# Another order of the opening in a fused attention and gated FFN kernel: the second tile joins at the sixth step, conversions rank above attention

## The chip, the cores and the metric

The kernel runs on one core of a Trainium2 chip. The metric is the device time of one execution in microseconds; the time of a kernel is the median of its runs. The engines are named as in the profile: PE (TensorE, matmuls), PEld (its weight loads), DVE (VectorE), ACT (ScalarE), POOL (GpSimd) and SP (SyncE, which issues every DMA here).

## The reference

Attention over keys and values that are averaged over groups of 8 positions, and behind it a gated FFN on the attention's output:

```python
B, H, S, D = 8, 8, 576, 64
k_p = k.reshape(B, H, 72, 8, D).mean(axis=3)          # 72 pooled keys
v_p = v.reshape(B, H, 72, 8, D).mean(axis=3)
scores = q @ k_p.T / sqrt(D)
attn = softmax(scores)                                 # sum + 1e-9
x = (attn @ v_p).transpose(0, 2, 1, 3).reshape(4608, 512)
out = ((x @ w_a) * (x @ w_b)) @ w_out                  # w_a, w_b: 512 x 1536, w_out: 1536 x 512
```

The weights come as 64-bit floating-point numbers; q, k and v as 32-bit ones.

## The kernel before, in words

**Precision.** Every operand of a matmul is split in a high part (a cast on ACT) and a low part (source minus high part, the helper `low_part`, L183, on DVE or POOL). A product is then three matmuls: high by high, high by low, low by high. For the FFN these are L610 to L612 (in) and L632 to L634 (out).

**Tiles and steps.** The 4608 rows of x are nine tiles of 512 columns (`NT`). A tile goes through 12 steps, one for each 128 of the 1536 hidden columns. A step has an "in" (`ffn_in`: 12 matmuls for psa with w_a, 12 for psb with w_b; ACT copies psa to h at L617, DVE multiplies it by psb at L567) and an "out" (`ffn_out`: 12 matmuls into the four accumulators acc). The product h is split in `split_gated` into hh (ACT, L580) and hl (DVE). The "out" of a step comes after the "in" of the next.

**Converting weights.** The weights' words are loaded and turned to 32-bit numbers in place by `convert_weights`, once for each of a, b, o and each of the 12 steps: two ACT operations (L225, L226), three DVE operations (L227, L231, L236), and the load of the next step's words between the last two. Conversion g may not start before step max(g - AHEAD, 0) of the first tile has begun (list `begun`, two slots later for b, four for o). `split_weight` then makes high (ACT, L262) and low part (L183; for a and b of tile 0 on DVE, otherwise on POOL) for each use, at most two of a weight at a time (`room`).

**The second tile.** Tile 1 uses the freshly converted weights of steps LAG to 11 together with tile 0, so that they are split only once for both. Those products h are "kept": stored to DRAM (`later`, L570) and fetched again (`fetch_gated`, L586) when tile 1's "out" steps are due. Steps 0 to LAG - 1 of tile 1 come afterwards, with splits of their own.

**Attention.** Rows are cut in 40 chunks of 128 or 64. `chunk(i)` loads and splits queries, makes scores on PE (L418 for the first nine chunks, L432 and L435 later, whose two parts DVE adds at L438), softmax (maximum L402, subtraction L403, exponential L452 on ACT, sum and reciprocal L454 to L456, scaling L458 mostly on POOL), splits the probabilities (pr, rem: L467, L469, POOL at L183), turns them on PE (ptr, L513, copied by ACT at L514), and multiplies them by the values (po, L548 to L551; xh at L559 and xl at L183). `load_keys(b)` and `load_values(b)` pool a batch's keys (L282, L293, L298) and values (L334, L339, L343, L354, L357, vrem at L183). The first four chunks make tile 0, the next five tile 1.

**The order.** It is planned in Python while the program is written. The FFN's instructions are issued in the list `order`. An "in" takes four slots, an "out" two (IN, OUT). In each slot `Chains.step` resumes the generators that are due, in order of rank, then one generator that waits for PE. A `yield n` lets a chain rest for n slots; `yield PE` queues it for PE. Where the FFN can't go on, `need` runs steps with up to GROUPS chains on PE each. The order of resumption is the order of instructions in each engine's queue; the engines then run by semaphores. Ranks are PRODUCTS, SPLITS, CHUNKS, WEIGHTS, KEYS (L131), the first ahead. Splits are started LEAD_A, LEAD_B, LEAD_O slots before their use, a fetch LEAD_H slots before. A chunk of tiles 2 to 8 is started CHUNK slots before a point spread evenly over the tile before; keys KEYS_AHEAD slots ahead of a chunk, values VALUES_AFTER slots after the keys.

**The opening.** Chunks of tile 0 start EARLY_GAP slots apart, those of tile 1 from SECOND_START on, SECOND_GAP apart; values, keys and conversions at VALUES_START, KEYS_START and WEIGHTS_START; a conversion's first arithmetic comes CONVERT_AFTER slots after its load. The FFN waits for all of tile 0's attention before its first step, and for all of tile 1's before tile 1's first "in":

```python
        for n, (kind, t, *where) in enumerate(order):
            if kind == "in":
                if t == 0:
                    begun.append(chains.now)
                need(lambda: have(t))
```

Of the kernel before, what the change touches and what calls it, by code (L numbers as in the profile page):

```python
# [55 lines left out]

SUMMED = 9

AHEAD = 2

GROUPS = 4


LAG = 4


IN, OUT = 4, 2
LEAD_A, LEAD_B, LEAD_O, LEAD_H = 5, 4, 6, 8


QUERY_GAP, PROBS_GAP, VALUE_GAP = 4, 2, 4
CHUNK = 34
SECOND_GAP, SECOND_START = 3, 14
KEYS_AHEAD, VALUES_AFTER = 18, 16


EARLY_GAP, VALUES_START, KEYS_START, WEIGHTS_START, CONVERT_AFTER = 1, 2, 8, 10, 5


class Chains:  # L80
# [9 lines left out]
    def mark(self, *what):  # L90
        self.done.add(what)

    def wait(self, *marks):
        while not all(m in self.done for m in marks if not isinstance(m[-1], int) or m[-1] >= 0):
            yield 1
# [26 lines left out]
def attn_moe_kernel(ctx: ExitStack, tc: tile.TileContext, q, k, v, vr, wa, wb, wo, out):  # L122
# [5 lines left out]
    chains = Chains()  # L128
    PE = Chains.PE
    mark, wait, done = chains.mark, chains.wait, chains.done  # L130
    PRODUCTS, SPLITS, CHUNKS, WEIGHTS, KEYS = ((x, 0) for x in range(5))  # L131

    def tmp(name, dtype=F32):
        return sb.tile([P, 512], dtype, tag="tmp", name=name, bufs=NTMP)
# [47 lines left out]
    def low_part(eng, lo, src, hi):  # L182
        eng.tensor_tensor(out=lo, in0=src, in1=hi.bitcast(F32), op=ALU.subtract)  # L183
# [23 lines left out]
    def convert_weights(name, j, first):  # L207
# [11 lines left out]
        for f in range(NF):  # L219
# [19 lines left out]

            step = max(f + 1 - AHEAD, 0)  # L240
            while len(begun) <= step or chains.now < begun[step] + 2 * j:
# [9 lines left out]
    def drop(*keys):  # L251
        for key in keys:
            del parts[key]
            held[key[0]] -= 1
# [53 lines left out]
    def load_values(b):  # L308
        vd = vdiag[b % 2]
        vrem = sb.tile([P, NG, 2, 2, D], F32R, tag="vrem", name=f"vrem_{b}")  # L310
        yield from wait(("keys", b, 2), ("values", b - 1))
        vp = sb.tile([P, NK + NG, D], F32, tag="vp", name=f"vp_{b}", bufs=1)
        for x0 in range(0, NK + NG, 2):
            if b == 0:
                vraw = [early_v[:, x, :] if x < NK else early_vr[:, x - NK, :] for x in (x0, x0 + 1)]
            else:
                if x0:
                    yield from wait(("vraw", b, x0 - 2))
                vraw = [sb.tile([P, S], F32, tag="kv", name=f"vraw_{b}_{x0 + j}")[:, :D * POOL] for j in range(2)]
                for j in range(2):  # L320
                    if x0 < NK:
                        nc.sync.dma_start(vraw[j], v[b, :, x0 + j, :])
                    else:
                        nc.sync.dma_start(vraw[j][:NR], vr[b, :, x0 + j - NK, :])
                yield 3
            for j in range(2):
                x, rows = x0 + j, P if x0 < NK else NR
                vv = vraw[j][:rows].rearrange("p (d j) -> p d j", j=POOL)
                if b == 0 and 0 < x < NK:
                    for n in (4, 2, 1):  # L330
                        to = vp[:rows, x].unsqueeze(2) if n == 1 else vv[:, :, :n]
                        nc.gpsimd.tensor_tensor(out=to, in0=vv[:, :, :n], in1=vv[:, :, n:2 * n], op=ALU.add)
                else:
                    nc.vector.tensor_reduce(out=vp[:rows, x], in_=vv, axis=AX.X, op=ALU.add)  # L334
            mark("vraw", b, x0)
            yield 1
        for e in range(2):
            r = slice(e * KM, e * KM + KM)
            nc.scalar.mul(vd[r, :, 0, r], vp[r, :NK], 1.0 / POOL)  # L339

        wide = tmp(f"vwide_{b}").rearrange("p (r j e d) -> p r (j e) d", r=NG, j=2, e=2)
        for r in range(NG):
            nc.vector.scalar_tensor_tensor(  # L343
                out=wide[:NR, r],
                in0=vp[:NR, NK + r].unsqueeze(1).broadcast_to([NR, 4, D]),
                scalar=1.0 / POOL,
                in1=mask[:NR].unsqueeze(2).broadcast_to([NR, 4, D]),
                op0=ALU.mult,
                op1=ALU.mult,
            )  # L350
        wide = wide.rearrange("p r c d -> p (r c d)")
        vrf = vrem.rearrange("p r j e d -> p (r j e d)")
        yield 1
        nc.scalar.copy(vrf[:NR], wide[:NR])  # L354
        for e in range(2):
            r = slice(e * KM, e * KM + KM)
            nc.vector.scalar_tensor_tensor(  # L357
                out=vd[r, :, 1, r],
                in0=vp[r, :NK],
                scalar=1.0 / POOL,  # L360
                in1=vd[r, :, 0, r].bitcast(F32),
                op0=ALU.mult,
                op1=ALU.subtract,
            )
        yield 1
        r = slice(2 * 4 * KR, NR)
        low_part(nc.vector, vrf[r], wide[r], vrf[r])
        yield 1
        vrems[b] = vrem
        mark("values", b)  # L370

    def chunk(i):
        b, o, n = flat[i]
        t, col = divmod(b * S + o, NT)
        first, soon = i < early, t < 2
# [11 lines left out]
        nc.scalar.copy(qh[:, :, :n], qraw[:, :, :n])  # L387
        yield 1
        low_part(nc.gpsimd if first else nc.vector, ql[:, :, :n], qraw[:, :, :n], qh[:, :, :n])
        yield 1 if soon else QUERY_GAP  # L390
        yield from wait(("probs", i - 2))


# [77 lines left out]
        low_part(nc.gpsimd, pr[:n, 1], s[:n, :, :KM], pr[:n, 0])  # L471
        low_part(nc.gpsimd, rem[:n, :, 1], sr, rem[:n, :, 0])
        mark("probs", i)
        yield 1 if soon else PROBS_GAP


        j = block_of[i]
# [47 lines left out]
        mark("turned", i)  # L525
        if i != members[-1]:
            return
        yield 1 if soon else VALUE_GAP
        yield from wait(("values", b))
        if t not in xtiles:  # L530
            xtiles[t] = [sb.tile([P, NK, NT], F32R, tag=x, name=f"{x}_{t}") for x in ("xh", "xl")]
# [58 lines left out]
    def need(ready):  # L590
        for _ in range(1000):
            if ready():
                return
            chains.step(GROUPS)
        raise RuntimeError("no progress")

    def ffn_in(t, f):
        x = t * NF + f
        xh, xl = xtiles[t]
        kept = t == 1 and f >= LAG  # L600
        for name in ("a", "b"):
# [4 lines left out]
            for kk in range(NK):  # L606
# [5 lines left out]
                nc.tensor.matmul(pt, wl[:, c], xh[:, kk], start=False, stop=(kk == NK - 1))  # L612
            if t or f < LAG:
                drop(key)
# [35 lines left out]
    for f in range(NF):  # L650
        order.append(("in", 0, f))
        if f >= LAG:
            order.append(("in", 1, f))
        if f:
            order.append(("out", 0, f - 1, f == 1, False))
    order.append(("out", 0, NF - 1, False, True))
    seconds = [*range(LAG, NF)]
    for f in range(LAG):
        order.append(("in", 1, f))
        if f:  # L660
            order.append(("out", 1, f - 1, False, False))
        order.append(("out", 1, seconds.pop(0), f == 0, False))
    order.append(("out", 1, LAG - 1, False, False))
    order += [("out", 1, f, False, f == NF - 1) for f in seconds]
# [8 lines left out]
    for kind, t, f, *_ in order:  # L673
        x = t * NF + f
# [7 lines left out]
    with tc.manual_schedule():  # L682
# [8 lines left out]
        for i in range(early):  # L691
            chains.start(chunk(i), (CHUNKS[0], i), EARLY_GAP * i)
        for i in range(early, sum(t < 2 for t in tile_of)):
            chains.start(chunk(i), (CHUNKS[0], i), SECOND_START + SECOND_GAP * (i - early))
        chains.start(load_values(0), KEYS, VALUES_START)
        chains.start(load_keys(1), KEYS, KEYS_START)
        chains.start(load_values(1), KEYS, KEYS_START + 1)
        for j, name in enumerate(("a", "b", "o")):
            chains.start(convert_weights(name, j, CONVERT_AFTER + 2 * j), WEIGHTS, WEIGHTS_START)
# [10 lines left out]
        for n, (kind, t, f, *_) in enumerate(order):  # L710
            x = t * NF + f
# [10 lines left out]
        for i in range(len(flat)):  # L722
            b, o, n = flat[i]
            t = tile_of[i]
            if t < 2:
                continue
            since = free if t == 2 else begin_of[t - 1]
            share = (b * S + o + n - t * NT) / NT
            begin_at = since + int((begin_of[t] - since) * share) - CHUNK
            plan.append((begin_at, chunk(i), (CHUNKS[0], i)))  # L730
            if i + 1 < len(flat) and flat[i + 1][0] > max(b, 1):
                plan.append((begin_at - KEYS_AHEAD, load_keys(b + 1), KEYS))
                plan.append((begin_at - KEYS_AHEAD + VALUES_AFTER, load_values(b + 1), KEYS))
# [60 lines left out]
```

## Time and profile before

| what | value |
|---|---|
| median of 3 runs | 1098.72 us (1096.58 to 1099.33) |
| profiled execution | 1099.94 us, span 1098.2 us |
| PE, PEld busy | 1036.8 us (94%), 860.6 us (78%) |
| DVE, ACT, POOL busy | 588.3, 516.3, 505.7 us |
| mean granted PE clock | 0.981 |

A row of the windows names a stretch of the span in us, then for each engine its busy time in it with the number of instructions, the granted clock (1 is full), the mean busy share of the DMA engines, and GB/s. A row of instructions in order of time has start, duration, engine, line, operation, operands and count, and in brackets the engine's idle time ahead of it with what ended it. A row of the groups has busy time and mean ns of one, then the idle time ahead. A "step" below is a step of a tile, a "slot" a slot of the planner.

### The profile page before, as it was taken

The page shows a single profiled execution, that of the slowest core. Times are in us where ns is not written, and L with a number is a line of the kernel's source. Part 1 is how long each engine was busy: PE and PEld are TensorE (multiplying, and loading weights), DVE is VectorE, ACT ScalarE, POOL GpSimd, SP SyncE. Part 2 cuts the span into 40 slices and gives each one's busy share as a digit, 9 for nine tenths or more (in the row PEclk, how much of TensorE's full clock was granted, in tenths as well). Part 3 has the DMA queues.
Part 4 walks back from the last instruction along what each step waited for, and adds up shares of the span by engine and source line. Part 5 has one row for each costly group of instructions (what it writes and reads, how often), then busy time and mean ns, then how long its engine had stood idle before and what let it go on. Part 6 is the DMA issues. An engine that isn't in the chain of part 4 may idle for free.

```text
span 1098.2 us, 13575 instructions
## 1 busy us (share of the span) xinstructions
PE 1036.8 (94%) x4964; PEld 860.6 (78%) x4964; DVE 588.3 (54%) x941; ACT 516.3 (47%) x1035; POOL 505.7 (46%) x425
## 2 busy tenths in 40 slices
PE   4577699999999999999999999999999999999998
PEld 4555588788878888888877888888887888888886
DVE  7879857764685345644566446543557343422112
ACT  3656535445454445544444445444544344443332
POOL 6213100036555554555455455554545555554442
PEclk9878899999999999999999999999999999999999
DMA  6354424413230002200140002100211010001001
GB/s 217 104 148 125 135 88 148 145 43 118 94 127 1 1 2 75 98 1 1 34 149 1 1 1 89 63 1 1 83 54 37 1 58 1 1 1 39 1 1 39
DMA packets 32178, 63.79 MB, mean 58 GB/s; under 512 B 7376, under 2 KB 7376, under 8 KB 32112
## 3 DMA queue, kind: packets, MB, share of 16 engines
q1 hardware_dynamic: 32112, 62.93, 17.9%
q8 instruction: 39, 0.64, 0.2%
q14 instruction: 27, 0.22, 0.1%
HBM read 51.38 MB, written 11.53 MB: 57 GB/s over the span
## 4 chain that ended last, share of the span: by engine, by line
PE 81%; DVE 11%; ACT 3%; DMA 3%; issue 2%; POOL 0%; SPq 0%; DVEq 0%; ACTq 0%; POOLq 0%
PE psa L610 8%; PE acc L632 8%; PE psb L610 8%; PE acc L634 8%; PE acc L633 8%; PE psa L612 8%; PE psa L611 8%; PE psb L612 8%; PE psb L611 8%; PE ptr L513 2%; PE psc L432 2%; DVE vp L334 1%; PE po L550 1%; PE po L548 1%; PE po L551 1%
## 5 line engine op out<-in xcount | busy, mean ns | idle before, releaser
L567 DVE TENSOR_TENSOR h<-psb,h 128x512 f32<-128x512 f32 x108 | 74.6, 690 | 322.0 <-PE psb L612 314.0
L183 POOL TENSOR_TENSOR jlb<-wb_raw,jhb 128x512 fp32r<-128x512 f32 x88 | 114.9, 1306 | 256.1 <-ACT jhb L262 256.1
L183 POOL TENSOR_TENSOR jlo<-wo_raw,jho 128x512 fp32r<-128x512 f32 x108 | 142.4, 1319 | 141.1 <-ACT jho L262 141.1
L617 ACT COPY h<-psa 128x512 f32<-128x512 f32 x108 | 63.5, 588 | 255.2 <-PE psa L612 241.5
L610 PE MATMUL psa<-xh,jha 128*128 128x512 f32 x432 | 175.5, 406 | 0.8 <-DVE xl L183 0.8
L610 PE MATMUL psb<-xh,jhb 128*128 128x512 f32 x432 | 171.8, 398 | 1.4 <-DVE h L567 1.4
L632 PE MATMUL acc<-jho,hh 128*128 128x512 f32 x432 | 172.1, 398 | 0.0
L611 PE MATMUL psa<-xl,jha 128*128 128x512 f32 x432 | 170.9, 396 | 0.0
L612 PE MATMUL psa<-xh,jla 128*128 128x512 f32 x432 | 170.8, 395 | 0.0
L634 PE MATMUL acc<-jho,hl 128*128 128x512 f32 x432 | 169.1, 392 | 0.0
L633 PE MATMUL acc<-jlo,hh 128*128 128x512 f32 x432 | 168.7, 391 | 0.0
L612 PE MATMUL psb<-xh,jlb 128*128 128x512 f32 x432 | 168.6, 390 | 0.0
L611 PE MATMUL psb<-xl,jhb 128*128 128x512 f32 x432 | 168.5, 390 | 0.0
L183 POOL TENSOR_TENSOR jla<-wa_raw,jha 128x512 fp32r<-128x512 f32 x88 | 120.5, 1370 | 77.1 <-ACT jha L262 69.9
L183 DVE TENSOR_TENSOR hl<-h,hh 128x512 fp32r<-128x512 f32 x100 | 92.5, 925 | 32.7 <-ACT hh L580 32.5
L580 ACT CAST hh<-h 128x512 fp32r<-128x512 f32 x100 | 62.2, 622 | 94.2 <-DVE h L567 91.6
L612 PEld LDWEIGHTS psa<-xh,jla 128*128 128x128 f32 x432 | 82.7, 191 | 18.0
L610 PEld LDWEIGHTS psa<-xh,jha 128*128 128x128 f32 x432 | 82.9, 192 | 15.9 <-DVE xl L183 1.0
L634 PEld LDWEIGHTS acc<-jho,hl 128*128 128x128 f32 x432 | 81.4, 188 | 17.6
L612 PEld LDWEIGHTS psb<-xh,jlb 128*128 128x128 f32 x432 | 81.1, 188 | 17.3
L610 PEld LDWEIGHTS psb<-xh,jhb 128*128 128x128 f32 x432 | 81.1, 188 | 17.2 <-DVE h L567 1.8
L611 PEld LDWEIGHTS psa<-xl,jha 128*128 128x128 f32 x432 | 83.0, 192 | 14.6
(102 smaller groups left out, 1701.8 us busy)
## 6 DMA issues: line engine op xcount, KB each, us to landing
out<-y SPq DMA_DIRECT2D x36, 256.0 KB, 2.2
kraw<-in_k SPq DMA_DIRECT2D x28, 288.0 KB, 3.6
qraw<-in_q SPq DMA_DIRECT2D x28, 256.0 KB, 3.7
vraw<-in_v SPq DMA_DIRECT2D x28, 256.0 KB, 3.0
words<-in_wa SPq DMA_DIRECT2D x12, 512.0 KB, 3.6
words<-in_wb SPq DMA_DIRECT2D x12, 512.0 KB, 3.5
words<-in_wo SPq DMA_DIRECT2D x12, 512.0 KB, 3.6
vraw<-in_vr SPq DMA_DIRECT2D x14, 192.0 KB, 2.8
```

The source lines that it names most:

```text
L183: eng.tensor_tensor(out=lo, in0=src, in1=hi.bitcast(F32), op=ALU.subtract)
L432: nc.tensor.matmul(pt[:n, :2 * hk], qh[:, g, :n], kd[:, g].rearrange("p w e s -> p (w e s)"), start=True, stop=False)
L513: nc.tensor.transpose(ptr[:rows, g, :n], src, ident[:n, :n])
L567: nc.vector.tensor_tensor(out=h, in0=pt, in1=h, op=ALU.mult)
L580: nc.scalar.copy(hh, h)
L610: nc.tensor.matmul(pt, wh[:, c], xh[:, kk], start=(kk == 0), stop=False)
L611: nc.tensor.matmul(pt, wh[:, c], xl[:, kk], start=False, stop=False)
L612: nc.tensor.matmul(pt, wl[:, c], xh[:, kk], start=False, stop=(kk == NK - 1))
L617: nc.scalar.copy(h, pt)
L632: nc.tensor.matmul(acc[c], hh[:, cs], wh, start=first, stop=False)
L633: nc.tensor.matmul(acc[c], hh[:, cs], wl, start=False, stop=False)
L634: nc.tensor.matmul(acc[c], hl[:, cs], wh, start=False, stop=last)
```

## The change

Constants of the order are changed, one pair of ranks is swapped, and three rests of the first chunks' chains are told apart for the first and the second tile. AHEAD goes from 2 to 1, GROUPS from 4 to 3, LAG from 4 to 5; LEAD_A, LEAD_O, LEAD_H from 5, 6, 8 to 3, 8, 6; CHUNK from 34 to 33; SECOND_GAP from 3 to 1; VALUES_AFTER from 16 to 14; EARLY_GAP, VALUES_START, KEYS_START, CONVERT_AFTER from 1, 2, 8, 5 to 2, 3, 6, 2. WEIGHTS ranks above CHUNKS. The turns of a chunk of tile 1 come SECOND_PROBS = 3 slots after the split of its probabilities, where it was 1. `load_values` rests between its operations in batches 2 to 7.

```diff
--- before.py
+++ after.py
@@ -56,25 +56,27 @@
 
 SUMMED = 9
 
-AHEAD = 2
-
-GROUPS = 4
-
-
-LAG = 4
+AHEAD = 1
+
+GROUPS = 3
+
+
+LAG = 5
 
 
 IN, OUT = 4, 2
-LEAD_A, LEAD_B, LEAD_O, LEAD_H = 5, 4, 6, 8
+LEAD_A, LEAD_B, LEAD_O, LEAD_H = 3, 4, 8, 6
 
 
 QUERY_GAP, PROBS_GAP, VALUE_GAP = 4, 2, 4
-CHUNK = 34
-SECOND_GAP, SECOND_START = 3, 14
-KEYS_AHEAD, VALUES_AFTER = 18, 16
-
-
-EARLY_GAP, VALUES_START, KEYS_START, WEIGHTS_START, CONVERT_AFTER = 1, 2, 8, 10, 5
+CHUNK = 33
+SECOND_GAP, SECOND_START = 1, 14
+KEYS_AHEAD, VALUES_AFTER = 18, 14
+
+SECOND_QUERY, SECOND_PROBS, SECOND_VALUE = 1, 3, 1
+
+
+EARLY_GAP, VALUES_START, KEYS_START, WEIGHTS_START, CONVERT_AFTER = 2, 3, 6, 10, 2
 
 
 class Chains:
@@ -128,7 +130,7 @@
     chains = Chains()
     PE = Chains.PE
     mark, wait, done = chains.mark, chains.wait, chains.done
-    PRODUCTS, SPLITS, CHUNKS, WEIGHTS, KEYS = ((x, 0) for x in range(5))
+    PRODUCTS, SPLITS, WEIGHTS, CHUNKS, KEYS = ((x, 0) for x in range(5))
 
     def tmp(name, dtype=F32):
         return sb.tile([P, 512], dtype, tag="tmp", name=name, bufs=NTMP)
@@ -332,6 +334,8 @@
                         nc.gpsimd.tensor_tensor(out=to, in0=vv[:, :, :n], in1=vv[:, :, n:2 * n], op=ALU.add)
                 else:
                     nc.vector.tensor_reduce(out=vp[:rows, x], in_=vv, axis=AX.X, op=ALU.add)
+                if b > 1:
+                    yield 1
             mark("vraw", b, x0)
             yield 1
         for e in range(2):
@@ -348,6 +352,8 @@
                 op0=ALU.mult,
                 op1=ALU.mult,
             )
+            if b > 1:
+                yield 1
         wide = wide.rearrange("p r c d -> p (r c d)")
         vrf = vrem.rearrange("p r j e d -> p (r j e d)")
         yield 1
@@ -362,6 +368,8 @@
                 op0=ALU.mult,
                 op1=ALU.subtract,
             )
+            if b > 1:
+                yield 2
         yield 1
         r = slice(2 * 4 * KR, NR)
         low_part(nc.vector, vrf[r], wide[r], vrf[r])
@@ -387,7 +395,7 @@
         nc.scalar.copy(qh[:, :, :n], qraw[:, :, :n])
         yield 1
         low_part(nc.gpsimd if first else nc.vector, ql[:, :, :n], qraw[:, :, :n], qh[:, :, :n])
-        yield 1 if soon else QUERY_GAP
+        yield (1 if first else SECOND_QUERY) if soon else QUERY_GAP
         yield from wait(("probs", i - 2))
 
 
@@ -471,7 +479,7 @@
         low_part(nc.gpsimd, pr[:n, 1], s[:n, :, :KM], pr[:n, 0])
         low_part(nc.gpsimd, rem[:n, :, 1], sr, rem[:n, :, 0])
         mark("probs", i)
-        yield 1 if soon else PROBS_GAP
+        yield (1 if t == 0 else SECOND_PROBS) if soon else PROBS_GAP
 
 
         j = block_of[i]
@@ -525,7 +533,7 @@
         mark("turned", i)
         if i != members[-1]:
             return
-        yield 1 if soon else VALUE_GAP
+        yield (1 if t == 0 else SECOND_VALUE) if soon else VALUE_GAP
         yield from wait(("values", b))
         if t not in xtiles:
             xtiles[t] = [sb.tile([P, NK, NT], F32R, tag=x, name=f"{x}_{t}") for x in ("xh", "xl")]
```

## The prediction

> **What bounds the kernel now.** I read the page first (engine shares, slices), then the windows of PE's stages, then PE's waits, then the instruction rows around each stall. From the page:
>
> ```profile
> span 1098.2 us, 13575 instructions
> PE 1036.8 (94%) x4964; PEld 860.6 (78%) x4964; DVE 588.3 (54%) x941; ACT 516.3 (47%) x1035; POOL 505.7 (46%) x425
> PE   4577699999999999999999999999999999999998
> DVE  7879857764685345644566446543557343422112
> ```
>
> PE is full except in the first five slices, where DVE stands at 6 to 9 tenths. The opening is one regime, all that follows another. The windows of stages, columns PE, PEld, DVE, ACT, POOL busy with counts, granted clock, DMA share, GB/s:
>
> ```profile
> 0.00:52.60 52.60, 27.10 (x144) 24.57 (x145) 43.10 (x79) 26.54 (x60) 25.52 (x35) 0.94 0.53 168
> 52.60:139.76 87.16, 64.60 (x291) 50.76 (x292) 71.64 (x120) 50.74 (x101) 19.93 (x18) 0.83 0.43 128
> 200.00:222.00 22.00, 20.62 (x93) 16.77 (x92) 16.64 (x29) 9.62 (x19) 1.31 (x1) 1.00 0.41 135
> 222.00:318.00 96.00, 95.84 (x472) 80.25 (x471) 59.44 (x100) 48.84 (x100) 48.38 (x38) 1.00 0.24 77
> 318.00:334.00 16.00, 14.14 (x66) 11.37 (x65) 14.41 (x21) 9.70 (x22) 9.42 (x9) 0.89 0.48 156
> 559.00:595.00 36.00, 32.71 (x163) 26.03 (x161) 25.57 (x40) 16.01 (x34) 17.36 (x15) 1.00 0.21 67
> 595.00:826.00 231.00, 231.00 (x1127) 193.71 (x1126) 114.19 (x184) 111.01 (x225) 124.30 (x102) 1.00 0.12 37
> 826.00:850.00 24.00, 21.45 (x111) 16.54 (x109) 18.31 (x26) 10.37 (x23) 11.39 (x10) 1.00 0.05 17
> 850.00:1093.80 243.80, 243.80 (x1148) 203.06 (x1148) 73.99 (x111) 98.14 (x189) 120.02 (x96) 1.00 0.03 12
> ```
>
> At 52.60 the first FFN step starts; about 139.56 the second tile joins (both rows below). Between them PE idles 87.16 - 64.60 = 22.56 us and runs at clock 0.83, while DVE is busy 71.64 of 87.16 (82%). Later PE is full but for four islands: 1.38 us in 200 to 222, 1.86 in 318 to 334, 3.29 in 559 to 595, 2.55 in 826 to 850; 318 to 334 also has clock 0.89, worth 16 x 0.11 = 1.76 us. One attention-free step of 36 matmuls costs 1009.57 - 1001.41 = 8.16 us, so a planner slot (a sixth) is 1.36 us; PE's instructions in order of time:
>
> ```profile
> 52.60 0.79 PE L610 MATMUL psa<-xh,jha 128*128 128x512 f32 x1 [0.77 <-DVE xl L183]
> 139.56 0.63 PE L610 MATMUL psa<-xh,jha 128*128 128x512 f32 x1
> 1001.41 0.39 PE L610 MATMUL psa<-xh,jha 128*128 128x512 f32 x1
> 1009.57 0.39 PE L610 MATMUL psa<-xh,jha 128*128 128x512 f32 x1
> ```
>
> What PE waits for (us in total, times, longest):
>
> ```profile
> PE ptr L513 <- ACT pr L467: 13.9, 4, 5.4
> PE psc L418 <- ACT p L514: 7.0, 3, 4.3
> PE psc L432 <- DVE s L438: 3.8, 4, 1.4
> ```
>
> The first two belong to the opening's attention, each a link of the chain scores, softmax, turn; the third to the islands.
>
> **The change part by part.**
>
> **Second tile joins at step five, not four; conversions run one step ahead, not two.** In the listed order the second tile's first "in" stands behind 5 "in" and 3 "out" of tile 0 (5x4 + 3x2 = 26 slots); after the change behind 6 and 4 (32 slots). So 36 more matmuls, 8.16 us of PE work, lie where PE now idles, and the second tile's attention gets 6 more slots. What DVE pays: the number of conversions ahead of the join. Now conversion g is released at the start of step g-2, after the change at g-1. Windows of L236, the last operation of a conversion, and of L567 (the product), DVE busy and counts:
>
> ```profile
> 0.00:52.60 52.60, 1.38 (x2) 0.94 0.53 168
> 52.60:139.76 87.16, 15.02 (x19) 0.83 0.43 128
> 52.60:139.76 87.16, 3.41 (x5) 0.83 0.43 128
> ```
>
> 2 + 19 = 21 conversions, three weights times seven (steps 0 to 6), precede the join: number 6 is released by step 4. After the change step 5 stands ahead of the join, and releases number 6 as the last. The conversions stay at 21. What DVE gains is one more split of a and b, one product, one split of the product, at the means of the groups by shape:
>
> ```profile
> L183 DVE TENSOR_TENSOR jla<-wa_raw,jha 128x512 fp32r<-128x512 f32 x12 | 8.2, 684 | 0.0
> L183 DVE TENSOR_TENSOR jlb<-wb_raw,jhb 128x512 fp32r<-128x512 f32 x12 | 9.6, 803 | 0.2 <-ACT jhb L262 0.2
> L567 DVE TENSOR_TENSOR h<-psb,h 128x512 f32<-128x512 f32 x108 | 74.6, 690 | 322.0 <-PE psb L612 314.0 <-ACT jho L262 4.4 <-ACT qh L387 2.0
> L183 DVE TENSOR_TENSOR hl<-h,hh 128x512 fp32r<-128x512 f32 x100 | 92.5, 925 | 32.7 <-ACT hh L580 32.5
> ```
>
> 0.684 + 0.803 + 0.690 + 0.925 = 3.10 us. If the join is set by DVE (82% busy), it comes 3.10 us later with 8.16 us more done: 5.06 us gained. Bounds: the whole 8.16 if the 3.10 fall into DVE's own idle time, zero if the stretch grows by a whole step. I take -5.1, as DVE's share is nearer to full. A conversion one step later has its data sooner, since its words load starts in the conversion before it; SP issues the same word loads. Its split is due three slots (4.1 us) after its release, and late by that only if DVE is jammed.
>
> **Smaller consequences of the fifth step.** One store and one fetch of h fewer (seven, not eight): off the path, zero. One more a and b split for tile 1, on POOL: 2 x 1.3 us where POOL is busy 48.38 of 96 (222 to 318); zero, and 2.6 us if that cover went. The fetches are issued two slots before their split, not four:
>
> ```profile
> back<-later SPq DMA_DIRECT2D x8, 256.0 KB, 4.6
> ```
>
> 2 slots are 2.72 us, so ACT can stand 1.88 us at the cast, with the next weight's cast queued behind it. Its user is four slots (5.4 us) off and cast and split take about 1.5 us, so this is covered; zero, and 7 x 1.88 = 13.2 us if nothing covers it.
>
> **Order up to the first step** (early chunks two slots apart, keys at 6, conversions after 2 instead of 5 and ranked above chunks, three PE groups instead of four in a wait, second-tile chunks at 14 to 18 instead of 14 to 26, their turns three slots behind their splits). No instruction is added; SP's loads of keys and words trade places. DVE is busy 43.10 of 52.60, so the order can win at most its 9.50 us of idle time. It can lose what is put ahead: three second-tile chunks, each with two maxima, two subtractions and a sum:
>
> ```profile
> L403 DVE TENSOR_TENSOR s<-psc,m 128x288 f32<-128x288 f32 x14 | 6.4, 457 | 0.9
> L402 DVE TENSOR_REDUCE m<-psc 128x4 f32<-128x288 f32 x14 | 6.3, 450 | 0.5 <-PE psc L418 0.4
> L454 DVE TENSOR_REDUCE z<-s 128x8 f32<-128x576 f32 x32 | 23.7, 742 | 0.8 <-ACT s L452 0.8
> ```
>
> 3 x (2 x 0.457 + 2 x 0.450 + 0.742) = 7.7 us. This is moved, not added, and comes back before the join; the three-slot gap of the turns spares PE a turn that arrives before its probabilities. I take zero between -9.5 and +7.7.
>
> **Value loads in pieces (batches 2 to 7).** DVE now gets their operations in pairs. DVE in the islands:
>
> ```profile
> 322.16 2.73 DVE L357 SCALAR_TENSOR_TENSOR vdiag<-vp,vdiag 64x256 fp32r<-64x256 f32 x2 [0.92 <-ACT vdiag L339]
> 571.77 1.47 DVE L334 TENSOR_REDUCE vp<-vraw 96x64 f32<-96x512 f32 x2 [3.41 <-DMA vraw<-in_vr]
> 830.88 1.77 DVE L183 TENSOR_TENSOR vrem<-vwide,vrem 32x512 fp32r<-32x512 f32 x1
> ```
>
> Behind each pair stand the reduction L438 that frees a scores bank, and the product. With yields between, these go first. 200 to 222 (1.38), 318 to 334 (1.86 + 1.76 of clock), and 826 to 850 without its second stall (2.55 - 1.14 = 1.41) sum to 6.41 us; I take all of it. The remaining 3.29 - 1.12 = 2.17 us at 559 to 577 follow a wait for data (3.41 us of DVE idle); the load keeps its three slots, so it stays. Bounds: zero, and 6.41 + 2.17 = 8.58.
>
> **Leads and phases.** a is split three slots ahead, not five, o eight, not six; chunks start one slot later, a phase shift of one sixth of a step. Same instructions. By slots, POOL now gets jlo, jla, jlb in a row, three slots to one before the "in". With 1.32 us each (row below) they fit their slots, and jla is done about one slot (1.36 us) early: zero. If a chunk's pr (1.3) and remainder push them, PE waits some tenths. What a long run on POOL does is seen at 585:
>
> ```profile
> 585.66 1.29 POOL L183 TENSOR_TENSOR jlb<-wb_raw,jhb 128x512 fp32r<-128x512 f32 x1
> 588.16 1.27 POOL L183 TENSOR_TENSOR pr<-s,pr 64x512 fp32r<-64x512 f32 x1
> 586.14 3.84 DVE L183 TENSOR_TENSOR hl<-h,hh 128x512 fp32r<-128x512 f32 x1 [0.69 <-ACT hh L580]
> 590.39 0.34 PE L432 MATMUL psc<-kdiag,qh 128*64 128x288 f32 x1 [1.12 <-DVE s L438]
> 845.16 0.35 PE L432 MATMUL psc<-kdiag,qh 128*64 128x288 f32 x1 [1.14 <-DVE s L438]
> L183 POOL TENSOR_TENSOR jlo<-wo_raw,jho 128x512 fp32r<-128x512 f32 x108 | 142.4, 1319 | 141.1 <-ACT jho L262 141.1
> ```
>
> hl took 3.84 us instead of 0.69 and PE stalled 1.12 us. The Trainium skill, page "SBUF — State Buffer", section "Who interferes with whom", says that a DVE instruction with two SBUF inputs and a GpSimd instruction that reads SBUF exclude each other for the whole instruction; by that rule the three splits in a row keep such DVE work waiting in every step, which speaks against this change, and the sum would be that of the last rival below instead of -11.5. The row agrees for this place; the product h, one of whose inputs is PSUM, has mean 690 over 108. I take zero because hl is due when the run of splits has ended; now it falls beside jlb.
>
> **Sum.** -5.1 - 6.4 = -11.5 us on the profiled execution's 1099.94 (span 1098.2 and 1.7 around it) gives 1088.4; its run lies 1.2 above the median 1098.72, and against that median I predict 1087.2.
>
> **The rivals.**
>
> *The opening only moves its idle time* (the second tile's last chain, not DVE, ends last at the join; the two opening waits, 13.9 and 7.0, speak for it; the 6 slots more for that chain against): -6.4, 1092.3.
>
> *The islands stay* (POOL runs or data, not pairs, make them): -5.1, 1093.6.
>
> *Nothing happens*: first step later by up to 7.7 and islands elsewhere: -11.5 + 7.7 = -3.8 at most, 1095 to 1099. DVE at 82% before 52.60 speaks for it.
>
> *More goes*: the step fits wholly into idle time (8.16), all value stalls (8.58) and the two run stalls (1.12 + 1.14): -19.0, 1079.7.
>
> *Slower: POOL runs stall every chunk.* Three splits in a row, with pr and its remainder ahead of them, hold DVE's subtraction L403 or ql, and through them L438: 1.12 us at each of 31 later chunks is +34.7 (40 chunks less the nine of the first two tiles); less 11.5, it is +23, 1122. It decides from 11 stalls on (11.5 / 1.12 = 10.3), and from 14 on the kernel is measurably slower. For it: the row at 586. Against: only two such stalls now, although POOL has such runs at each chunk, and DVE has half its time free (114.19 of 231.00).
>
> **How the numbers follow.** Forecast 0.38 (its own range 1083 to 1091), more 0.10, opening moves 0.13, islands stay 0.11, nothing 0.12, slower 0.16. Faster by over 0.3% (3.3 us, about what a measurement tells from no change): 0.38 + 0.10 + 0.13 + 0.11 = 0.72; same 0.12; slower 0.16. The range 1077 to 1104 leaves out half of the slower case and a little of "more".
>
> **What would show it.** Right: 7 conversions of each weight and 6 products before the second tile's first matmul; that matmul about 3 us later than 139.56 if the first step starts near 52.6; PE full at the value loads of batches 2, 3 and 7; PE-free stretches still at the fifth batch's value load. Wrong: a first step after 57; hl or L403 with means above 1.5 us and PE waits on L438 at most chunks; a wait of L612 for jla in each step; seven ACT waits for fetched h in tile 1's second half with PE idle behind them.

## The result, and the profile after

The changed kernel takes 1070.55 us (median of 4 runs, 1068.14 to 1071.28) where the kernel before took 1098.10: ratio 0.9746, 95% interval 0.9725 to 0.9767, 27.6 us gone. Predicted were 1087.2 and a range of 1077 to 1104. The profiled execution's span is 1069.4 us, against 1098.2. Two single executions, one each of the kernels with one-input operations and with SECOND_PROBS 5 below, took about 2600 us; the ratios leave them out.

The page of the changed kernel (engine shares, then slices of the span):

```profile
PE 1029.1 (96%) x4964; PEld 855.9 (80%) x4964; DVE 622.7 (58%) x941; ACT 515.1 (48%) x1037; POOL 520.8 (49%) x427
PE   4678999999999999999999999999999999999998
DVE  7997967955674455644676456654668444423222
```

The same 4964 matmuls and 941 DVE instructions run. DVE is even busier, by 34 us; that costs nothing once PE is full from the fifth slice on. Where the time came from shows in the starts of three steps. PE in order of time in the changed kernel: first step, second tile's first step, third tile's first step:

```profile
50.24 0.50 PE L618 MATMUL psa<-xh,jha 128*128 128x512 f32 x1 [0.44 <-DVE xl L185]
130.94 0.39 PE L618 MATMUL psa<-xh,jha 128*128 128x512 f32 x1
297.91 0.39 PE L618 MATMUL psa<-xh,jha 128*128 128x512 f32 x1
```

And the third tile's first step in the kernel before:

```profile
317.11 0.39 PE L610 MATMUL psa<-xh,jha 128*128 128x512 f32 x1
```

The first step comes 2.4 us earlier (50.24, not 52.60). The join comes 8.6 us earlier (130.94, not 139.56) although one step more (8.16 us) lies ahead of it: 16.8 us won there. At the third tile 19.2 us are won, and the rest of the span gives 9.6 more. So the opening brought 16.8, forecast 5.1, and all that follows 12.0, forecast 6.4; this is between two profiled executions, 28.8 us apart. About 1 us of the opening's share belongs to that execution of the kernel before: two kernels below that differ from it only in later value loads (the rests, the one-input operations) start their first step at 51.75 and 51.82 us and the second tile at 138.03 and 138.68.

Windows of the changed kernel, cut at these starts (columns as before):

```profile
50.24:130.94 80.70, 67.95 (x326) 53.51 (x327) 70.97 (x117) 52.44 (x109) 23.10 (x20) 0.89 0.42 127
130.94:297.91 166.97, 166.69 (x785) 138.58 (x784) 115.19 (x183) 84.31 (x165) 54.18 (x43) 1.00 0.35 111
297.91:1065.30 767.39, 766.78 (x3711) 638.55 (x3709) 393.57 (x562) 352.25 (x708) 418.91 (x331) 1.00 0.10 32
```

Ahead of the join DVE is busy 88%, not 82%, and PE idles 12.75 us, not 22.6. After it PE idles 0.28 + 0.61 us: all four islands are gone. What PE waits for between first step and join, in the changed kernel:

```profile
PE ptr L521 <- ACT p L522: 4.4, 4, 2.4
PE ptr L521 <- DVE s L411: 3.8, 2, 2.3
PE psc L426 <- DVE ql L185: 2.6, 1, 2.6
```

And in the kernel before:

```profile
PE ptr L513 <- ACT pr L467: 9.5, 2, 5.4
PE psc L418 <- ACT p L514: 4.8, 2, 4.3
PE psc L418 <- DVE s L403: 3.2, 1, 3.2
```

The turns' wait for their own probabilities (ptr for pr), 9.5 us in two pieces, is gone from this stage.

### The profile page after: what moved, and what is told of

It is laid out like the page before. It is cut to its first block, busy times and chain, and to the rows that moved or that the text cites. A ratio compares the mean times of both kernels' runs of the same rounds, so it can differ in the third digit from the quotient of the medians.

```text
span 1069.4 us, 13397 instructions
## 1 busy us (share of the span) xinstructions
PE 1029.1 (96%) x4964; PEld 855.9 (80%) x4964; DVE 622.7 (58%) x941; ACT 515.1 (48%) x1037; POOL 520.8 (49%) x427
## 4 chain that ended last, share of the span: by engine, by line
PE 88%; DVE 7%; ACT 3%; issue 1%; DMA 0%; POOL 0%; SPq 0%; DVEq 0%; ACTq 0%; POOLq 0%
PE acc L640 9%; PE psa L618 9%; PE acc L642 9%; PE psb L618 9%; PE acc L641 9%; PE psa L620 9%; PE psa L619 9%; PE psb L620 9%; PE psb L619 9%; PE ptr L521 2%; PE psc L440 2%; PE po L558 1%; PE po L559 1%; PE psc L443 1%; PE po L557 1%; PE po L556 1%
## 5 line engine op out<-in xcount | busy, mean ns | idle before, releaser
L618 PE MATMUL psa<-xh,jha 128*128 128x512 f32 x432 | 173.2, 401 | 0.4 <-DVE xl L185 0.4
L185 POOL TENSOR_TENSOR jla<-wa_raw,jha 128x512 fp32r<-128x512 f32 x89 | 134.4, 1510 | 8.5 <-ACT jha L264 8.5
L185 DVE TENSOR_TENSOR hl<-h,hh 128x512 fp32r<-128x512 f32 x101 | 106.6, 1055 | 28.8 <-ACT hh L588 28.1
L185 POOL TENSOR_TENSOR jlb<-wb_raw,jhb 128x512 fp32r<-128x512 f32 x89 | 118.0, 1326 | 0.1
L185 DVE TENSOR_TENSOR ql<-qraw,qh 128x512 fp32r<-128x512 f32 (+1 forms) x36 | 41.6, 1157 | 90.0 <-ACT qh L395 90.0
```

What stands on the lines that cost most here:

```text
L618: nc.tensor.matmul(pt, wh[:, c], xh[:, kk], start=(kk == 0), stop=False)
```

## The experiments

Each ratio is to runs of the kernel before on the same chip. The changed kernel's is 0.9746. A thousandth is 1.1 us.

**Pieces of the change put into the kernel before.**

The fifth step alone:

```diff
-AHEAD = 2
+AHEAD = 1
-LAG = 4
+LAG = 5
```

> The kernel before with LAG 5 and AHEAD 1 alone. The step theory (the opening's 16.8 us at the join come from one more step of tile 0 being done in PE's idle time, with the conversions held to one step ahead): 1084 to 1090 us, second tile's first matmul at 131 to 135 us, islands after 200 us as before. The order theory (they come from the order of attention, its gaps and the rank of conversions): 1095 to 1098.

Measured: 0.9999 (0.9988 to 1.0011), 1096.83 us. The time is the order theory's. At the join something is won all the same: it comes at 139.88 us, not the 131 to 135 of the step theory, but with one step more (8.16 us) done, so 7.8 us are won there, about half of the 16.8. Yet the third tile starts at 314.92, only 2.2 us earlier than before. The gain was given back around 210 us; PE in that kernel, then its window (PE busy, clock, DMA share, GB/s):

```profile
214.70 0.61 PE L432 MATMUL psc<-kdiag,qh 128*128 128x288 f32 x1 [4.09 <-DVE s L438]
```

```profile
200.00:220.00 20.00, 15.91 (x63) 0.85 0.30 102
```

The island of 1.38 us has become one of 4.09, at the value load of batch 2, with a clock of 0.85 in this window. DVE is busy 17.55 of these 20 us, with conversions of weights beside the load, and POOL only 1.50: here L438 stands behind much work, not behind POOL. AHEAD and LAG were only ever changed together, so their shares are open.

The opening's order alone (all constants of the opening, the rank, the turns):

> The kernel before with the opening's order alone: GROUPS 3, SECOND_GAP 1, EARLY_GAP 2, VALUES_START 3, KEYS_START 6, CONVERT_AFTER 2, conversions ranked above chunks, SECOND_PROBS 3; LAG, AHEAD, leads and value loads as before. The step theory: 1094 to 1098 us (the first step 2.4 us earlier and no more). The order theory: 1082 to 1090, the second tile's first matmul 8 to 16 us earlier than 139.56.

Measured: 0.9911 (0.9892 to 0.9929), 1086.18 us; second tile's first matmul at 126.27, 13.3 us earlier (2.3 of them are the first step's earlier start, 50.28). The order theory holds. Three experiments divide it. The later turns:

```diff
-        yield 1 if soon else PROBS_GAP
+        yield (1 if t == 0 else 3) if soon else PROBS_GAP
```

> The kernel before with SECOND_PROBS 3 alone: the turns of tile 1 come three slots behind the split of their probabilities. Turns theory: 1085 to 1090 us, the two waits of ptr for pr after 90 us (9.5 us together) gone or under 2 us, second tile's first matmul at 128 to 132. Rank theory: 1095 to 1099, PE waits for something else at the same places.

Measured: 0.9926 (0.9911 to 0.9940), 1088.67 us, as the turns theory wants. Its PE waits between first step and join:

```profile
PE ptr L513 <- ACT p L514: 8.0, 4, 3.9
PE ptr L513 <- DVE s L403: 3.6, 2, 2.7
```

No ptr waits for pr there any more, and the second tile starts at 128.75, 10.8 us earlier; PE idles 13.20 us between first step and join, not 22.56. The two waits in the kernel before, with PE's rows around them:

```profile
98.14 0.39 PE L634 MATMUL acc<-jho,hl 128*128 128x512 f32 x1
102.62 0.75 PE L513 MATMUL ptr<-ident,pr 128*128 128x128 f32 x4 [4.09 <-ACT pr L467]
103.17 0.76 PE L632 MATMUL acc<-jho,hh 128*128 128x512 f32 x1
124.26 0.28 PE L418 MATMUL psc<-kdiag,ql 128*128 128x144 f32 x1
126.92 0.39 PE L612 MATMUL psb<-xh,jlb 128*128 128x512 f32 x1
132.70 0.75 PE L513 MATMUL ptr<-ident,pr 128*128 128x128 f32 x4 [5.39 <-ACT pr L467]
```

The first turn stood in the middle of an "out" whose matmuls had been running until 98.14, and held the rest of it 4.09 us. The second is another case: from 126.92 to the join PE has nothing but the second tile's own turns and products, so no ready work stood behind that turn. It was late because the tile's last scores had come only at 124.26. With later turns the scores of the next chunks go ahead of them on PE; the last scores in that kernel:

```profile
106.55 0.28 PE L418 MATMUL psc<-kdiag,ql 128*128 128x144 f32 x1
```

The softmax behind them then runs under FFN steps. This holds throughout: in the seven kernels with three slots the last scores ahead of the join come at 103.7 to 107.4 us, in the nine with one slot at 115.1 to 124.3.

The rank alone:

```diff
-    PRODUCTS, SPLITS, CHUNKS, WEIGHTS, KEYS = ((x, 0) for x in range(5))
+    PRODUCTS, SPLITS, WEIGHTS, CHUNKS, KEYS = ((x, 0) for x in range(5))
```

> The kernel before with conversions ranked above chunks, nothing else. Rank theory (the 11 us of the opening's order come from conversions going first on ACT and DVE): 1084 to 1089 us. Turns theory (they come from turns no longer queued on PE ahead of their probabilities): 1096 to 1099, and the two waits of ptr for pr after 90 us, 4.1 and 5.4 us, stay.

Measured: 1.0019 (1.0008 to 1.0029), 1099.04 us: a small loss. The rank theory falls.

The earlier starts, gaps and GROUPS alone:

> The kernel before with GROUPS 3, SECOND_GAP 1, EARLY_GAP 2, VALUES_START 3, KEYS_START 6 and CONVERT_AFTER 2, without the new rank and without the later turns. Turns theory: within 3 us of before (1094 to 1099), first step at 50 to 52. Start theory (what remains of the opening's order is here): 1090 to 1093.

Measured: 0.9964 (0.9950 to 0.9979), 1093.56 us. This falls in the gap between the two expectations, 0.4 us from the one and 0.6 from the other, so neither holds; which of the six constants counts was not tried. The single effects -8.1, +2.1 and -4.0 us sum to -10; together they gave -9.8.

The rests in the value loads alone:

> The kernel before with the rests in the value loads of batches 2 to 7 alone. The pieces theory (the islands come from DVE pairs of the value loads): 1087 to 1091 us, PE idle in 200 to 222, 318 to 334, 559 to 595 and 826 to 850 together under 2 us instead of 9.1. The phase theory (they come from where POOL's and ACT's splits fall against the chunks): 1096 to 1099, islands stay.

Measured: 0.9992 (0.9980 to 1.0004), 1095.77 us. The pieces theory falls, by itself: PE still stalls, 3.15 us at 583 and 3.15 at 840. Why shows at 576 us, DVE in that kernel:

```profile
576.46 3.13 DVE L345 SCALAR_TENSOR_TENSOR vwide<-vp,mask 96x256 f32<-96x256 f32 x1
579.51 0.68 DVE L183 TENSOR_TENSOR hl<-h,hh 128x512 fp32r<-128x512 f32 x1
580.12 2.97 DVE L361 SCALAR_TENSOR_TENSOR vdiag<-vp,vdiag 64x256 fp32r<-64x256 f32 x1
583.02 0.81 DVE L444 TENSOR_REDUCE s<-psc 64x144 f32<-64x288 f32 x2
```

POOL meanwhile:

```profile
576.77 1.29 POOL L183 TENSOR_TENSOR jlb<-wb_raw,jhb 128x512 fp32r<-128x512 f32 x1
578.02 1.28 POOL L183 TENSOR_TENSOR jlo<-wo_raw,jho 128x512 fp32r<-128x512 f32 x1
579.27 2.04 POOL L183 TENSOR_TENSOR pr<-s,pr 64x512 fp32r<-64x512 f32 x1
```

A single operation, not a pair, takes 3.13 us, and ends 0.3 us after POOL's jlo does; the next takes 2.97. L444 (the old L438) comes only then, and PE has waited 3.15 us. Parting the pairs does not help while each part waits out a run of POOL.

Leads and phases alone (LEAD_A 3, LEAD_O 8, LEAD_H 6, CHUNK 33, VALUES_AFTER 14):

> The kernel before with LEAD_A 3, LEAD_O 8, LEAD_H 6, CHUNK 33 and VALUES_AFTER 14 alone. The pieces theory: 1097 to 1100 us, islands stay. The phase theory: 1087 to 1091, islands together under 2 us. The rival of POOL runs from the prediction: over 1102, PE waits on L438 at many chunks.

Measured: 0.9941 (0.9922 to 0.9959), 1089.58 us. The time is the phase theory's, and three of the islands are gone; one is left and has grown from 1.86 to 3.65 us, DVE and then PE in that kernel:

```profile
318.08 2.88 DVE L357 SCALAR_TENSOR_TENSOR vdiag<-vp,vdiag 64x256 fp32r<-64x256 f32 x2
```

```profile
321.50 0.35 PE L432 MATMUL psc<-kdiag,qh 128*64 128x288 f32 x1 [3.65 <-DVE s L438]
```

Here one operation takes 1.4 us, and it is the pair that holds L438. So each half of the change lacks the other. Which of the five settings moves the waits was not tried. Both together:

> The kernel before with leads, CHUNK and VALUES_AFTER of the change and the rests in the value loads, the opening as before. Need-both theory (leads shorten one operation's wait, rests part the pairs): islands after 140 us under 1 us, 1082 to 1086. Additive theory (the single effects, -6.5 and -0.9): 1089 to 1090, an island left at 300 to 330.

Measured: 0.9877 (0.9859 to 0.9895), 1084.50 us, against -7.4 us for the sum of the single effects; PE idles under 0.5 us in every 20 us window after the join's. The need-both theory holds.

**What makes the islands.** The three DVE operations of the value loads that read two SBUF tiles were replaced by reductions of one; here one of the three:

```diff
+            if b > 1:
+                with nc.allow_low_precision(reason="sum of one"):
+                    nc.vector.tensor_reduce(out=vd[r, :, 1, r], in_=vp[r, :NK].unsqueeze(3), axis=AX.X, op=ALU.add)
+                continue
             nc.vector.scalar_tensor_tensor(
                 out=vd[r, :, 1, r],
...
```

> The kernel before, with the three DVE operations of the value loads of batches 2 to 7 that read two SBUF tiles (vwide L343, the low part of vdiag L357, the remainder vrem) replaced by reductions over one element of the same shapes, which read one tile; the low parts of the values are left out by that, and vwide's mask and scale. Lock theory (these operations stand still while POOL runs without a gap, and L438 and PE stand behind them): none of them over 0.8 us, the islands at 318 to 334 and 826 to 834 gone, 1091 to 1094 us; the stalls behind hl (2.3 us together) and the waits for vr data stay. Volume theory (DVE has too much in front of L438): 1096 to 1099, islands as before.

Measured: 0.9925 (0.9906 to 0.9943), 1090.43 us, a little more than the lock theory asked. The stalls at 325 and 833 us are gone, and so is the one of 2.17 us at 577 that the prediction put down to data: DVE still waits 2.57 us for them there, but no PE stall follows. The island at 212 stays (1.36 us), so these operations do not make it; POOL is busy only 1.31 us from 200 to 222 in the kernel before. The tiles' rows (duration ns min/median/max) of that kernel:

```profile
L365 DVE TENSOR_REDUCE vdiag<-vp x12: 399/408/417, 223.1 to 822.7; 64x256 fp32r<-64x256 f32 x12
L344 DVE TENSOR_REDUCE vwide<-vp x12: 403/405/408, 221.7 to 820.3; 96x256 f32<-96x256 f32 x12
```

In the kernel before, vdiag takes up to 1415 ns in batches 2 to 7, vwide up to 1494. The operation still reading two tiles keeps its wait; DVE, then PE:

```profile
832.66 3.85 DVE L183 TENSOR_TENSOR hl<-h,hh 128x512 fp32r<-128x512 f32 x1 [0.69 <-ACT hh L594]
```

```profile
836.93 0.34 PE L446 MATMUL psc<-kdiag,qh 128*64 128x288 f32 x1 [1.14 <-DVE s L452]
```

This shows it for operations of equal shape: two SBUF inputs stand still behind POOL, one does not. That it is the inputs and not the kind of operation shows in the kernel before, where the product h (L567) has the operation and shape of hl, but reads PSUM for one input: all 108 take 674 to 693 ns, while hl goes from 631 to 3854. The Trainium skill, page "SBUF — State Buffer", section "Who interferes with whom", says that a DVE instruction with two SBUF inputs contends with a GpSimd instruction that reads SBUF, and that a reduction never contends; the rows agree, with at most 417 ns for the reductions above.

**Pieces of the change taken out of the changed kernel.**

Without the rests in the value loads:

> The changed kernel without the rests in the value loads. Phase theory (the islands come from DVE operations with two SBUF inputs that stand in front of L438 while POOL runs several operations without a gap, and the leads moved these runs): 1070 to 1073 us. Need-both theory (the rests matter once the opening is shorter): 1075 to 1080, islands in the value loads of batches 2 and 3.

Measured: 0.9844 (0.9824 to 0.9863), 1079.42 us: the need-both theory. Its islands are at 204 (2.49 us) and 312 us (3.65). At 312 it is a pair of vdiag again (2.88 us); at 204 DVE is full of conversions, products and the value load, and POOL is busy only 1.29 us from 190 to 206.

With the old leads, CHUNK and VALUES_AFTER:

> The changed kernel with LEAD_A 5, LEAD_O 6, LEAD_H 8, CHUNK 34, VALUES_AFTER 16 as before. Phase theory: 1077 to 1081 us, islands of 3 us at the value loads where jlb, jlo and pr run on POOL without a gap. Pieces theory: 1070 to 1073.

Measured: 0.9904 (0.9882 to 0.9927), 1087.88 us, more than the phase theory asked. Of the 17 us, 4.8 are lost at the join (135.74, not 130.94). Behind it PE stalls 1.56 us at 207, 3.15 at 574 and 3.15 at 832. The second of these, and the window around it (PE, clock, DMA share, GB/s):

```profile
574.25 0.50 PE L440 MATMUL psc<-kdiag,qh 128*64 128x288 f32 x1 [3.15 <-DVE s L446]
576.41 0.63 PE L618 MATMUL psa<-xh,jha 128*128 128x512 f32 x1
576.84 0.63 PE L619 MATMUL psa<-xl,jha 128*128 128x512 f32 x1
```

```profile
560.00:580.00 20.00, 16.85 (x71) 0.83 0.10 29
```

The stall is followed by matmuls 0.43 us apart instead of 0.23 (8.16 us for 36). In the 20 us from the end of this stall the clock is 0.86, so 20 x 0.14 = 2.8 us more; from the end of the one at 832 it is 0.91, 1.8 us more. Join, stalls and clock together are 4.8 + 7.9 + 4.6 = 17.3 us.

With LAG 4 and AHEAD 2:

> The changed kernel with LAG 4 and AHEAD 2 as before. Step theory (a step of tile 0 in PE's idle time, worth 8 us at the join in the first experiment but given back in a larger island, counts once the islands are gone): 1077 to 1080 us. Rival (with turns no longer in PE's way the step has no idle time left to fill): 1069 to 1072.

Measured: 0.9800 (0.9783 to 0.9818), 1076.07 us: the step theory. The fifth step is worth 5.9 us once nothing takes it back. The second tile joins at 128.02 there and at 130.94 in the changed kernel, 2.9 us later with 8.16 us more done; PE idles 17.28 us between first step and join there, 12.75 in the changed kernel.

With SECOND_PROBS 1:

> The changed kernel with SECOND_PROBS 1 as before. Turns theory: 1077 to 1080 us, PE waits of ptr for pr behind the first step over 5 us. Rival (the step more of FFN work ahead of the join hides the turns by itself): 1069 to 1073.

Measured: 0.9795 (0.9781 to 0.9808), 1074.69 us: the later turns are worth 5.4 us here. The time lies between the theories, and the waits that grow are not those expected: ptr waits for pr stay at 5.7 us over the whole span, against 5.5 in the changed kernel, while scores wait for p 6.4 us instead of 2.5. As in the kernel before, it is the scores that come later: the last ahead of the join at 115.10 us, not 105.98, and the second tile at 133.62, not 130.94.

With SECOND_PROBS 5:

> The changed kernel with SECOND_PROBS 5. Turns theory: 1069 to 1073 us if three slots already cover the wait; 1066 to 1068 if the waits of ptr that are left (3.8 and 4.8 us) are turns queued too early; over 1074 if the attention of tile 1 now ends too late for the join.

Measured: 0.9805 (0.9786 to 0.9824), 1075.03 us. More room loses 6.5 us; three slots lie between two worse values. That tile 1's attention then ends too late would fit; no trace shows it, so this stays argued.

With chunks ranked above conversions:

> The changed kernel with chunks ranked above conversions again. If the rank costs here as it did in the kernel before (+2 us alone): 1068 to 1069.5 us. If conversions that run only one step ahead need to go first: 1073 to 1080, with PE waiting for jla or jlb of tile 0's steps.

Measured: 0.9776 (0.9763 to 0.9790), 1072.01 us. By ratio the new rank is worth 3.3 us here, by the medians as they stand 1.5; the intervals overlap (up to 0.9767, from 0.9763), so a gain is not clear of noise. Neither expectation holds. No version tried beats the changed kernel.

The pieces close the account: the opening's order 9.8 us, leads and rests together 13.5 and the fifth step in the changed kernel 5.9 are 29.2 us, where the whole change gives 27.9 by its ratio.

## Why the prediction was wrong

The direction was right. Two terms that were set to zero failed, and one that was counted rested on half a mechanism.

*Order up to the first step, zero.* This is the step that failed first. I bounded what the order does ahead of the first step, where it brought 2.4 us at most, and closed the part with "spares PE a turn that arrives before its probabilities" at no price. The price stood in a row I had quoted, ptr waiting for pr 13.9 us, of which 9.5 lie behind the first step. The later turns alone gave 8.1 us, the whole order 9.8, and not only through that wait: they let the second tile's scores go ahead, the last at 106.55 us instead of 124.26.

*Leads and phases, zero.* Alone they gave 6.5 us, and taking them out costs 17. I had shown that hl stood 3.84 us behind a POOL run, and used it only for the rival that new runs would slow the kernel. The same row said that the present runs were part of the islands. The rival's cause was right and its sign wrong: POOL does hold DVE longer on the whole, but not ahead of L438, for which PE waits 0.2 us in all. Groups of the changed kernel:

```profile
L185 DVE TENSOR_TENSOR hl<-h,hh 128x512 fp32r<-128x512 f32 x101 | 106.6, 1055 | 28.8 <-ACT hh L588 28.1
L575 DVE TENSOR_TENSOR h<-psb,h 128x512 f32<-128x512 f32 x108 | 74.1, 686 | 191.9 <-PE psb L620 186.2 <-ACT qh L395 2.6 <-ACT jho L264 2.3
L411 DVE TENSOR_TENSOR s<-s,m 128x576 f32<-128x576 f32 x25 | 28.6, 1146 | 0.9
```

Means of 1055 and 1146 ns for hl and the subtraction against 925 and 791 before, and no PE wait from them; the product h, one of whose inputs is PSUM, keeps 686. The long single waits are fewer: the longest hl takes 1.79 us instead of 3.85. At the fifth batch's value load, where I expected an island to stay, DVE in the changed kernel:

```profile
564.08 1.37 DVE L363 SCALAR_TENSOR_TENSOR vdiag<-vp,vdiag 64x256 fp32r<-64x256 f32 x1
565.38 0.80 DVE L446 TENSOR_REDUCE s<-psc 64x144 f32<-64x288 f32 x2
566.21 1.26 DVE L363 SCALAR_TENSOR_TENSOR vdiag<-vp,vdiag 64x256 fp32r<-64x256 f32 x1
567.50 0.81 DVE L446 TENSOR_REDUCE s<-psc 64x144 f32<-64x288 f32 x2
```

These operations still wait, about one POOL instruction each, but a reduction goes between them.

*Value loads in pieces, -6.4.* Alone they gave 0.9 us, within the noise; in the changed kernel 10.8. I took the pair for the cause because the rows show two instructions as one line. What was long at 322 to 324, 574 and 830 was each wait for POOL; the 1.38 us at 212 were neither (1.05 stay with the rests alone, 1.36 with the one-input operations). That the terms could be added was itself a step that failed: rests and leads each left a stall that the other removes.

*Second tile at step five, -5.1.* Right in size in the changed kernel (5.9), zero by itself, since the island at 210 us grew to 4.09. The path was wrong, so the size is partly luck. I let DVE's work set the join. The kernel before ends that stretch with the second tile's own chain (the rows from 124.26 on, above), as the first rival said, which took it as a reason for no gain. And DVE did not pay 3.10 us: with the fifth step it works 42.43 + 70.97 = 113.4 us to the join, without it (LAG 4 and AHEAD 2) 42.98 + 69.80 = 112.8. The sixth product comes after the second tile's first matmul (131.14 us), and only 6 conversions of o, not 7, come ahead of it.

*Smaller consequences, zero.* Held: ACT's list of waits in the changed kernel has none for a fetched h. As forecast, its waits for weights' words (3.4, 1.7 and 1.4 us for o, b and a in the kernel before) are gone.

## What to carry to other kernels

Where one planner orders all engines' queues, price each rest by the wait it removes and by what it lets go ahead, and look both up by engine: an instruction queued too early on PE cost its wait to the matmuls behind it, and put off the scores on which the next stage hung. When an operation on the critical path stands behind slow ones, compare each one's duration with its usual duration before blaming their number, and look at what the neighbour engine runs at that moment. Terms that share a stall do not add: test a piece both put in alone and taken out of the whole.

## What the runs showed of the hardware that was not expected

The wait is not for one POOL instruction but can span several: hl took 3.84 us beside jlb, jlo and pr run without a gap, vwide 3.13 us beside the end of a scaling, jlb and jlo. A PE stall can cost more than itself, by an amount that varies: in the 20 us from the end of the four stalls of 3.15 us (two with the rests alone, two with the old leads) the granted clock was 0.85 to 0.92, so 1.6 to 3.0 us more each. Shorter stalls go both ways. In the kernel before, the clock was 0.91 behind the stall of 1.86 us at 326 and 1.00 behind the other five of 1.1 to 2.2 us; with the fifth step alone it was 1.00 behind the same stall (1.85 us at 323).
